# Weight sums loaded before a chunk ends, results made in pieces, relus put behind the next copy

## The chip, the cores and the metric

The kernel runs on one core of a Trainium2 chip. The metric is device time in microseconds, as the median of several runs. All inputs and outputs are 32-bit floats (the weights of the last two blocks arrive as 64-bit patterns and are narrowed on the chip).

## The reference, cut to what matters

Three blocks follow each other on a batch of 4 sequences of 576 rows and 512 features:

```
attn = thresholded softmax attention, 8 heads of 64                # block 1
X = real(fft(fft(x, axis=1), axis=2)); u = x + X                   # block 2
un = (u - mean(u)) / sqrt(var(u) + 1e-6)
y = u + relu(un @ w_ch1) @ w_ch2          # 512 -> 2048 -> 512
gate = sigmoid(causal conv of 5 taps over y)                       # block 3
out = (gate * (y @ w_val)) @ w_out
```

The change is in block 2's last line. The rows of all sequences, 4 x 576 = 2304, are cut there into chunks.

## The kernel before, in words

**Number format.** Every factor of a product is kept as a high and a low part, and a product is three passes: high x high, low x high, high x low. So a value that enters TensorE is first split: ScalarE makes the high part with a copy, and VectorE the rest with a subtraction.

**Chunks.** `CHUNKS` has 512, 384, 512, 512 and 384 rows. Chunk 0 is woven into the attention by a planner (`Loom`), which simulates the engines' clocks and picks which piece of work is emitted next. From chunk 1 on the order is written out in `mlp` (L1618 to L1676). Each engine runs its instructions in the order of emission, and so does SP, which issues nearly all DMAs. The planner goes on beside that with side work: the weight sums described below (`g_combine`), and narrowing the weights of block 3 (`g_load`, `g_convert`, L281 to L291).

**An ordinary chunk** (1 and 4) goes through 16 blocks of hidden features. `emit_h` (L1121) multiplies one block of `w_ch1` with the split rows `un`, then ScalarE takes the relu out of PSUM as `hh` and VectorE its remainder `hl`. `emit_c` (L1138) multiplies `w_ch2` with these into four PSUM accumulators, one block behind.

**A fast chunk** (2 and 3, `g_fast`, L1237) takes hidden blocks in pairs, in 8 steps, and saves products by a scheme in the manner of Strassen and Winograd: the chunk's rows are cut in two halves, and seven products of 256 columns do what eight would. The right-hand sides (`b11`, `b21`, `b22`, `t1` to `t4`, made by `g_blocks` on VectorE as differences and split by `split_block`, L1221) stay for the whole chunk; each set takes the room of a tile that stood for something else before. The left-hand sides are blocks of `w_ch1` and four sums of them, `s1` to `s4`. `g_combine` makes the sums during chunk 1 and stores them to DRAM. `fetch` (L1231) brings them back on SP, into a ring of five slots. One step has the products x (b11), y (b21), x (t2), zz (t1), x (t3), zz (b22), x (t4), where x and zz gather several products in one PSUM tile. Between these, ScalarE copies intermediate values out of PSUM (`copied`, L1286), VectorE adds (`added`, L1290), and `relu` (L1295) puts one instruction on ScalarE and one on VectorE. `fill` (L1246) puts 8 groups of three matmuls for `w_ch2` between the products; they belong to the step before, so the first step has none, and the last step's follow at the chunk's end. In the last step of chunk 2, `renew` splits each right-hand side for chunk 3 as soon as its last product is emitted.

**The norm.** The mean and variance of the next chunk are worked out beside the current one by a generator (`g_norm`, then `g_var`, L1056 to L1101), which `advance_norm` (L1585) moves on by one step when a due time is reached. The due times are counted on an estimate of TensorE's progress. In a fast chunk it is called once after each yield of `g_fast`, in an ordinary one before a fast chunk twice per block. Its scratch tiles come from a pool of four buffers (`cs`, L1018). Chunk 1's end forces it on until `centred`, and then splits all seven right-hand sides for chunk 2 (L1661 to L1665).

**A chunk's result** (`finish`, L1150): for each of four row groups of features, VectorE multiplies the accumulator with the norm's factor into a tile of the pool of the relus (two buffers), POOL adds the residual (`load_res`), and SP stores each run of rows to DRAM (two runs in chunks 1 to 3). It stands at once behind the chunk's last matmuls, ahead of the next chunk. Chunk 4 then starts block 3's gate: it loads rows of y through SP and runs the convolution on VectorE, between the blocks (`start_gate`, L1714).

## Time and profile before

| What | us |
|---|---|
| median of 3 runs (872.08 to 877.37) | 873.7 |
| the profiled execution, its own time | 876.9 |
| its span, first to last instruction | 875.1 |
| TensorE busy in it (94%) | 821.1 |
| VectorE busy (72%) | 631.7 |
| ScalarE busy (52%) | 452.4 |
| GpSimd busy (45%) | 396.2 |
| mean granted TensorE clock, as a share of full speed | 0.982 |

Times in the rows are microseconds from the span's start unless a view gives ns. PE is TensorE's matmuls, PEld its weight loads, DVE VectorE, ACT ScalarE, POOL GpSimd, SPq the queue that issues DMAs. A name like `hl<-ct,hh` is what an instruction writes and reads, by the tile's name at allocation: `cx` and `ct` are the kernel's temporaries in a fast chunk, `raw` and `unh`, `unl` also the right-hand sides, and `mlp_xu` the ring of fetched sums. Chunk 1 lies at 427 to 495, chunk 2 to 603, chunk 3 to 699, chunk 4 to 773.

### The profile page before, as it was taken

The page shows a single profiled execution, that of the slowest core. Times are in us where ns is not written, and L with a number is a line of the kernel's source. Part 1 is how long each engine was busy: PE and PEld are TensorE (multiplying, and loading weights), DVE is VectorE, ACT ScalarE, POOL GpSimd, SP SyncE. Part 2 cuts the span into 40 slices and gives each one's busy share as a digit, 9 for nine tenths or more (in the row PEclk, how much of TensorE's full clock was granted, in tenths as well). Part 3 has the DMA queues.
Part 4 walks back from the last instruction along what each step waited for, and adds up shares of the span by engine and source line. Part 5 has one row for each costly group of instructions (what it writes and reads, how often), then busy time and mean ns, then how long its engine had stood idle before and what let it go on. Part 6 is the DMA issues. An engine that isn't in the chain of part 4 may idle for free.

```text
span 875.1 us, 14989 instructions
## 1 busy us (share of the span) xinstructions
PE 821.1 (94%) x5164; PEld 663.7 (76%) x5164; DVE 631.7 (72%) x1370; ACT 452.4 (52%) x947; POOL 396.2 (45%) x456
## 2 busy tenths in 40 slices
PE   8989999999899999999999759997999989999998
PEld 6555566566555668888899758986799889998996
DVE  7999999889989997888688635656533466627740
ACT  5787777776777766544452325334423314234432
POOL 4557865895698476664443030303211111066421
PEclk9999999999999999999999969998999999999999
DMA  6376365456725389769146266646543132253111
GB/s 209 104 226 212 103 191 177 169 162 216 244 101 176 120 295 370 240 231 384 67 182 233 68 198 191 196 148 207 157 149 100 55 102 91 79 199 108 61 47 62
DMA packets 76459, 145.00 MB, mean 166 GB/s; under 512 B 14296, under 2 KB 24536, under 8 KB 76384
## 3 DMA queue, kind: packets, MB, share of 16 engines
q1 hardware_dynamic: 69040, 120.20, 40.6%
q0 software_dynamic: 7200, 23.86, 8.8%
q8 instruction: 41, 0.67, 0.3%
q14 instruction: 34, 0.28, 0.1%
q10 hardware_dynamic: 144, 0.00, 0.0%
HBM read 104.17 MB, written 39.86 MB: 165 GB/s over the span
## 4 chain that ended last, share of the span: by engine, by line
PE 60%; DVE 20%; issue 7%; ACT 6%; POOL 4%; DMA 2%; SPq 1%; DVEq 0%; POOLq 0%; ACTq 0%
PE c L1261 7%; DVE neg L766 6%; PE c L1147 6%; PE h L1131 6%; DVE p L783 6%; PE o L1776 5%; PE h L1496 5%; PE c L1532 5%; PE v L1758 5%; PE x L1271 4%; PE s L701 4%; PE f L458 3%; ACT e L772 2%; PE t L803 2%; PE zz L1271 2%
## 5 line engine op out<-in xcount | busy, mean ns | idle before, releaser
L791 POOL TENSOR_SCALAR p<-p,su 128x576 f32<-128x576 f32 x144 | 109.6, 771 | 86.8 <-DVE su L718 77.5
L772 ACT ACTIVATE e<-s,neg 128x576 f32<-128x576 f32 x144 | 102.2, 742 | 50.9 <-DVE neg L766 44.3
L783 DVE SCALAR_TENSOR_TENSOR p<-s,thr,e 128x576 f32<-128x576 f32 x144 | 112.5, 815 | 8.7 <-DVE thr L711 0.5
L766 DVE TENSOR_REDUCE neg<-s 128x1 f32<-128x576 f32 x144 | 102.5, 747 | 5.9 <-PE s L701 5.3
L701 PE MATMUL s<-kt,qt 64*128 64x288 f32 (+1 forms) x640 | 99.1, 441 | 6.9 <-DVE p L783 5.7
L701 PEld LDWEIGHTS s<-kt,qt 64*128 64x128 f32 (+1 forms) x640 | 46.0, 176 | 46.5 <-issue 16.1
L803 PE MATMUL t<-ident,p 128*128 128x128 f32 x464 | 68.9, 280 | 9.3 <-ACT m L820 6.6
L803 PEld LDWEIGHTS t<-ident,p 128*128 128x128 f32 x464 | 50.5, 140 | 30.7 <-issue 13.2
L291 POOL TENSOR_TENSOR ct<-raw 128x512 fp32r<-128x512 f32 x24 | 26.3, 1095 | 101.2 <-DVE raw L287 81.8
L458 PE MATMUL f<-m,v 128*64 128x320 f32 (+1 forms) x512 | 69.5, 411 | 0.0
L820 ACT ACTIVATE m<-t 128x512 f32<-128x512 f32 x116 | 65.6, 598 | 1.7 <-PE t L803 0.8
L1134 ACT ACTIVATE hh<-h 128x384 fp32r<-128x384 f32 x32 | 15.7, 490 | 76.8 <-PE h L1131 76.6
L458 PEld LDWEIGHTS f<-m,v 128*64 128x64 f32 x512 | 33.8, 137 | 27.3 <-ACT m L820 3.5
L1147 PE MATMUL c<-hl,w1h 128*128 128x384 f32 x128 | 43.6, 340 | 2.3 <-DVE hl L1135 2.3
L1156 POOL TENSOR_TENSOR res<-ht,res 128x512 f32<-128x512 f32 (+1 forms) x20 | 23.2, 1195 | 48.4 <-DVE ht L1155 48.4
L1147 PE MATMUL c<-hh,w1h 128*128 128x384 f32 x128 | 43.4, 339 | 0.0
L1147 PE MATMUL c<-hh,w1l 128*128 128x384 f32 x128 | 43.3, 339 | 0.0
L1732 DVE SCALAR_TENSOR_TENSOR acc<-ypad,cw,acc 128x288 f32<-128x288 f32 x96 | 43.0, 518 | 0.0
L1761 DVE TENSOR_TENSOR gvf<-v,gate 128x288 f32<-128x288 f32 x30 | 13.7, 456 | 39.2 <-PE v L1758 39.2
L1135 DVE SCALAR_TENSOR_TENSOR hl<-h,hh 128x384 fp32r<-128x384 f32 x32 | 17.8, 556 | 31.4 <-ACT hh L1134 31.4
L283 ACT ACTIVATE cx<-cx,wide_bias 128x512 int32<-128x512 int32 x40 | 28.9, 721 | 13.7 <-DVE cx L281 13.6
L1261 PE MATMUL c<-hh,w1h 128*128 128x512 f32 x88 | 34.8, 395 | 1.0 <-ACT hh L1299 1.0
(343 smaller groups left out, 2226.6 us busy)
## 6 DMA issues: line engine op xcount, KB each, us to landing
raw<-in_moe_w_ch POOLq DMA_DIRECT2D x32, 512.0 KB, 6.0
mlp_xu<-s SPq DMA_DIRECT2D x64, 256.0 KB, 3.6
qt<-in_q SPq DMA_DIRECT2D x15, 576.0 KB, 4.9
kt<-in_k SPq DMA_DIRECT2D x15, 432.0 KB, 3.6
s<-raw SPq DMA_DIRECT2D x12, 512.0 KB, 2.6
ypad<-y_d SPq DMA_DIRECT2D x16, 288.0 KB, 3.0
out<-os SPq DMA_DIRECT2D x18, 256.0 KB, 2.0
v<-in_v SPq DMA_DIRECT2D x16, 256.0 KB, 2.6
```

The source lines that it names most:

```text
L458: PE.matmul(out=f[h * 64:h * 64 + 64, 0:n], lhsT=w, rhs=r, start=(t == 0), stop=(t == 4))
L701: PE.matmul(out=s[o, c, 0:HALF], lhsT=qt[w, hh, q], rhs=kt[w, 2 if h == 2 and hh else hh], start=True, stop=True)
L766: DVE.tensor_reduce(out=neg[u][:, j, 0:1], in_=sc[g][:, :, 0:HALF], axis=AX.XY, op=ALU.max, negate=True)
L772: ACT.activation(e, sc[g][:, :, 0:HALF], AF.Exp, bias=neg[u][:, j, 0:1], scale=1.0)
L783: DVE.scalar_tensor_tensor(out=p_view(g).rearrange("p (a b) -> p a b", a=2), in0=sc.pop(g)[:, :, 0:HALF], scalar=thr[u][:, j:j + 1], in1=e ...
L791: POOL.tensor_scalar(out=v, in0=v, scalar1=ssum[u][:, j:j + 1], scalar2=1.0, op0=ALU.mult, op1=ALU.mult)
L803: PE.matmul(out=f[:, t, :], lhsT=pv[:, t * 128:(t + 1) * 128], rhs=ident, is_transpose=True, start=(t == 0), stop=(t == 3))
L820: ACT.activation(o, fv, AF.Copy)
L1131: PE.matmul(out=f[:, 0:n], lhsT=ww[:, k * 128:(k + 1) * 128], rhs=x[:, k, 0:n], start=(i == 0), stop=(i == 3 * KB - 1))
L1147: PE.matmul(out=ch[c][o][:, 0:n], lhsT=ww[:, o * 128:(o + 1) * 128], rhs=x, start=(at_ == 0 and i == 0), stop=(at_ == FB - 1 and i == 2))
L1261: PE.matmul(out=ch[c][o][:, 0:n], lhsT=ww[:, o * 128:(o + 1) * 128], rhs=y[:, 0:n], start=(first and i == 0), stop=(last and i == 2))
L1271: PE.matmul(out=f[:, 0:m], lhsT=ww[:, k * 128:(k + 1) * 128], rhs=x[:, k], start=(first and i == 0), stop=(i == 5), skip_group_check=not f ...
```

## The change

- `g_var` waits a due time of 1,400 behind each of four squares, where it waited 2,000 behind each second one.
- `finish` becomes a generator, `g_finish`, that yields ahead of each of its four pieces. Its product goes into a scratch tile of the norm's pool. Behind chunks 1 and 2 it is not run at once: the next chunk, a fast one, takes one piece at every second yield of its first step. The planner and the norm do nothing in that chunk until yield 14, early in its second step. Behind chunks 0, 3 and 4 it still runs at once.
- In `g_fast`, `renew` becomes `settle`, and is called only behind products that are followed by a copy out of PSUM, or an addition from it into a temporary. Three of the four relus of a step are put on a list (`later`) and emitted there, behind the next such copy; the splits for the next chunk come behind them, in the order in which their products ended.
- At the last block of chunk 1 the norm is forced on to `centred`, and b11, b21 and t2 are split, ahead of that block's matmuls. The other four splits stay ahead of the last `emit_c`, and `fetch(5)` follows them there.

```diff
@@ g_var
                 ACT.activation(sq[k], z[:, k], AF.Square)
-                if k % 2:
-                    yield 2000.0
+                yield 1400.0
@@ finish
+            for _ in g_finish(c):
+                pass
+
+        def g_finish(c):
             n = CHUNKS[c]
             acc, u, r = ch.pop(c), res.pop(c), rs.pop(c)
             for k in range(KB):
-                t = f32(got["h"].tile([128, NM], F32R, tag="h" + "hl"[k % 2], name="ht"))[:, 0:n]
+                yield
+                t = scratch(n)
                 DVE.tensor_tensor(out=t, in0=acc[k][:, 0:n], in1=r, op=ALU.mult)
@@ g_fast
-            def renew():
+            later = []
+
+            def settle():
+                while later:
+                    relu(*later.pop(0))
                 while over:
-                    name = over.pop()
+                    name = over.pop(0)
                     if end and c + 1 in FAST:
                         split_block(c + 1, name)
...
                 product(x, a11, "b11", True)
                 copied(x, tmp[0])
-                renew()
+                settle()
                 yield
                 y = ps_f.tile([128, 512], F32, tag="f", name="y")
                 product(y, a12, "b21", True)
-                relu(added(y, tmp[0]), 2 * p, 0)
-                renew()
+                added(y, tmp[0])
+                later.append((tmp[0], 2 * p, 0))
                 yield
                 fill(1)
-                renew()
                 yield
                 product(x, s2, "t2", False)
                 copied(x, tmp[1])
+                settle()
                 fetch(k0 + 6)
-                renew()
...
                 product(z, s4, "b22", False)
-                relu(added(z, tmp[1]), 2 * p, 1)
+                added(z, tmp[1])
+                later.append((tmp[1], 2 * p, 1))
                 fetch(k0 + 9)
-                renew()
...
                 product(x, a22, "t4", False)
-                relu(x[:, 0:m], 2 * p + 1, 0)
-                renew()
+                settle()
+                later.append((x[:, 0:m], 2 * p + 1, 0))
...
+            settle()
             rest.append(lambda: fill(2 * KB))
@@ the loop over chunks
-                for m in g_fast(c):
+                for n, m in enumerate(g_fast(c)):
+                    if n % 2 == 1 and next(left, "end") != "end":
+                        continue
+                    if n < 14:
+                        continue
                     loom.run(until=loom.now["PE"])
...
                 rest.pop()()
-                finish(c)
+                left = g_finish(c)
+                if c + 1 not in FAST:
+                    finish_rest(left)
                 continue
...
             for n, j in enumerate(js):
+                if c + 1 in FAST and n == FB - 1:
+                    while not centred:
+                        advance_norm(c, True)
+                    loom.run(lambda: ("combined", FB // 2 - 1) in loom.done)
+                    for name in ("b11", "b21", "t2"):
+                        split_block(c + 1, name)
                 emit_h(c, j)
...
                 if c + 1 in FAST:
-                    for name in ("b11", "b21", "t2", "t1", "t3", "b22", "t4"):
+                    for name in ("t1", "t3", "b22", "t4"):
                         split_block(c + 1, name)
+                    fetch(5)
...
-            finish(c)
+            left = g_finish(c)
+            if c + 1 not in FAST:
+                finish_rest(left)
```

## Rows read from the trace of the kernel before

**Rows 1.** Waits of TensorE, 495 to 785: us in total, times, longest.
```profile
PE x L1271 <- DMA mlp_xu<-s: 11.7, 1, 11.7
PE x L1271 <- ACT cx L1288: 8.4, 5, 4.4
PE x L1271 <- DVE raw L1226: 2.9, 1, 2.9
PE c L1147 <- DVE hl L1135: 2.3, 1, 2.3
```

**Rows 2.** Timeline of the SP queue at chunk 1's end: start, us, line, tiles, count.
```profile
480.67 5.65 SPq L1016 DMA_DIRECT2D res<-u_d  x8
...
504.61 4.03 SPq L1158 DMA_DIRECT2D y_d<-res  x8
508.81 2.52 SPq L1234 DMA_DIRECT2D mlp_xu<-s  x5
```

**Rows 3.** Stretches: length, busy of PE, PEld, DVE, ACT, POOL; clock; DMA share; GB/s.
```profile
488.40:495.35 6.95, 6.94 (x40) 6.53 (x38) 3.55 (x7) 1.58 (x4) 1.03 (x1) 1.00 0.00 0
495.35:513.27 17.92, 2.81 (x12) 2.34 (x13) 10.77 (x19) 5.70 (x11) 4.57 (x5) 0.60 0.35 102
513.27:519.60 6.33, 6.33 (x30) 6.33 (x31) 1.35 (x2) 2.23 (x5) 2.40 (x2) 0.53 0.92 304
710.10:713.50 3.40, 3.40 (x11) 3.40 (x12) 3.40 (x6) 0.00 (x0) 0.00 (x0) 0.55 0.00 0
```

**Rows 4.** Timeline of TensorE: first fill of chunk 2; chunk 3's first product and first fill.
```profile
521.05 0.40 PE L1261 MATMUL c<-hh,w1h 128*128 128x512 f32 x1
...
602.78 0.40 PE L1271 MATMUL x<-raw,w0h 128*128 128x256 f32 x2
...
617.13 0.50 PE L1261 MATMUL c<-hh,w1h 128*128 128x512 f32 x1 [0.98 <-ACT hh L1299]
```

**Rows 5.** Chain that ended last, one product in chunk 2: start, us, matmuls.
```profile
560.05 0.71 PE zz L1271 x6
```

**Rows 6.** Timeline across chunk 1's end, with idle time before and its releaser.
```profile
488.01 0.73 ACT L283 ACTIVATE cx<-cx,wide_bias 128x512 int32<-128x512 int32 x1 [0.96 <-DVE cx L281]
...
488.45 0.63 PE L1034 MATMUL mean<-cs,ones 128*128 128x512 f32 x2
...
493.81 2.48 DVE L1053 TENSOR_TENSOR z<-z,mean 128x512 f32<-128x512 f32 x4
...
495.81 0.51 PE L1271 MATMUL x<-raw,w0h 128*128 128x256 f32 x2 [0.46 <-ACT raw L1225]
...
497.65 0.63 ACT L1225 ACTIVATE raw<-cs 128x512 fp32r<-128x512 f32 x1 [0.70 <-DVE cs L1217]
...
498.74 1.29 DVE L1226 TENSOR_TENSOR raw<-z,raw 128x512 fp32r<-128x512 f32 x2
```

**Rows 7.** Timeline behind chunk 3: POOL's four additions, a remainder in chunk 4.
```profile
697.83 5.04 POOL L1156 TENSOR_TENSOR res<-ht,res 128x512 f32<-128x512 f32 x4 [27.09 <-DVE ht L1155]
...
709.50 0.55 DVE L1135 SCALAR_TENSOR_TENSOR hl<-h,hh 128x384 fp32r<-128x384 f32 x1
```

**Rows 8.** Single lines: ns minimum/median/maximum, first and last start, shapes.
```profile
L1155 DVE TENSOR_TENSOR ht<-c,nr x20: 547/691/692, 424.7 to 774.8; 128x512 f32<-128x512 f32 x12, 128x384 f32<-128x384 f32 x8
...
L1292 DVE TENSOR_TENSOR cx<-y,cx x16: 408/424/426, 504.8 to 683.3; 128x256 f32<-128x256 f32 x16
...
L1299 ACT ACTIVATE hh<-cx x20: 399/418/421, 505.3 to 678.8; 128x256 fp32r<-128x256 f32 x20
...
L1300 DVE SCALAR_TENSOR_TENSOR hl<-ct,hh x12: 412/425/3199, 518.7 to 689.6; 128x256 fp32r<-128x256 f32 x12
```

**Rows 9.** Timeline of VectorE and POOL in the first steps of chunks 2 and 3.
```profile
505.84 0.92 DVE L1300 SCALAR_TENSOR_TENSOR hl<-cx,hh 128x256 fp32r<-128x256 f32 x1 [0.61 <-ACT hh L1299]
...
613.09 3.20 DVE L1300 SCALAR_TENSOR_TENSOR hl<-ct,hh 128x256 fp32r<-128x256 f32 x1 [0.62 <-ACT hh L1299]
...
613.47 2.53 POOL L1083 TENSOR_TENSOR cs<-cs 128x512 f32<-128x512 f32 x2
```

More of the change, by code (lines that the diff above doesn't have):

```diff
@@ L1342, in g_fast @@
                 added(x, tmp[2])
+                settle()
                 fetch(k0 + 8)
-                renew()
                 yield
@@ L1347, in g_fast @@
                 relu(tmp[2], 2 * p + 1, 1)
-                renew()
                 yield
                 product(z, s4, "b22", False)
-                relu(added(z, tmp[1]), 2 * p, 1)
+                added(z, tmp[1])
+                later.append((tmp[1], 2 * p, 1))
                 fetch(k0 + 9)
-                renew()
                 yield
                 fill(1)
-                renew()
                 yield
                 product(x, a22, "t4", False)
-                relu(x[:, 0:m], 2 * p + 1, 0)
-                renew()
+                settle()
+                later.append((x[:, 0:m], 2 * p + 1, 0))
                 yield
                 fill(3)
-                renew()
                 yield
@@ L1366, in g_fast @@
                     q += [group(p, jx, 2 * p + i, o) for o in range(KB)]
+            settle()
             rest.append(lambda: fill(2 * KB))
@@ L1616, in mlp, with finish_rest @@
         gated = False
+        def finish_rest(g):
+            for _ in g:
+                pass
+        left = iter(())
         arena()
```

## The prediction

> **What bounds the kernel now.** I read the waits of TensorE first, then the SP queue, then the stretches and the timelines around the boundaries between chunks. TensorE is the engine that sets the end: in chunks 1 to 4 it hardly waits, and what it does wait for stands nearly all at boundaries [rows 1]. The reader is to see three places.
> - Chunk 1 to 2. The first weight sum is fetched only after the eight stores of chunk 1's result, because all of them stand on SP in order: stores from 504.61, fetches from 508.81 [rows 2], and TensorE sits 11.7 us for the landing. Before that it sat 2.9 us for a split. The clock then falls: granted 0.60 while it idles and 0.53 in the 6.33 us of work behind it, near the lower of its two levels, against 1.00 before [rows 3]. The first fill of the second step starts at 521.05 [rows 4].
> - Chunk 2 to 3. From the first product at 602.78 to the first fill at 617.13 are 14.35 us [rows 4]. An unfilled step is seven products of 0.71 us [rows 5], so 5.0; 4.4 of the rest is one wait for a copy out of PSUM that ScalarE made late.
> - Chunk 3 to 4. One wait of 2.3 us for the remainder of a relu [rows 1], with the clock at 0.55 for the 3.4 us behind it [rows 3].
>
> **The change part by part.**
>
> **Loads and splits ahead of chunk 1's end.** Everything that the loads need is now forced ahead of the last hidden block of chunk 1, and its planner comes later than before: with a due time of 1,400 behind each of four squares, where there were two of 2,000, counting the due times through chunk 1's 16 blocks puts the column mean's inputs at the sixteenth block, not the fourteenth. So they are emitted behind a conversion step that ends on ScalarE at 488.74 [rows 6]. Then a ScalarE copy (0.63, as for a split) and a two-input subtraction on VectorE (0.65, half of the pair of 1.29) make them: 490.0. TensorE would have started the mean at 488.45, so it waits 1.6. After the mean's 0.63 come, in order on VectorE, the centring (2.48), four differences (4 x 0.65) and three remainders of splits (3 x 0.65): 490.7 + 2.48 + 2.6 + 1.95 = 497.7. Only then comes the last hidden block's remainder, 0.55 [rows 7]: 498.3. Behind it on VectorE wait the four other splits and a few conversion instructions; behind it on TensorE stands the last output block. TensorE works at 0.174 us a matmul (6.95 for 40, [rows 3]); the 26 matmuls from there to that block's second are done by about 495.2, so it waits some 3.1 us more and leaves chunk 1 at 500.1, where it now starts chunk 2 at 495.81 [rows 6]. That is a loss of 4.3. In return SP has nothing ahead of the five fetches but the residual's loads, which are out by 486.3 [rows 2]; from the first issue to the end of TensorE's wait were 513.27 - 508.81 = 4.5 us [rows 2, 3], so they are there by 495, and the 11.7 goes.
>
> **The result in pieces.** The first step of chunks 2 and 3 now holds, on VectorE, three additions (0.42), three remainders (0.43) and four products of the pieces (0.55 at 384 columns, 0.69 at 512) [rows 8]: 4.75 or 5.3 us. VectorE starts when two products are done (1.5 us) and stands about 1.6 us for ScalarE: 1.1 for the second copy and the first relu, and 0.5 for the second relu, at 0.42 each [rows 8] and a tenth for a signal. So the first fill can start 7.9 (8.4) us after the first product. The norm waits until step two, where its squares took turns with the first step; that costs nothing, since the counted due times still put the last difference of chunk 3 just ahead of the last step.
> The pieces' additions on POOL now lie beside the remainders. A remainder took 0.92 in place of 0.43 beside such an addition, and 3.20 beside two others, ending with the second of them [rows 9]. The nearest row is the first, since it has the same POOL instruction: 0.5 for each of two remainders, 1.2 with some for the third. The ends are 0 and 3 x 2.8 = 8.3 per chunk. The Trainium skill, "SBUF — State Buffer", section "Who interferes with whom", speaks against this place: a VectorE instruction with two SBUF inputs and a GpSimd one that reads SBUF shut each other out for one whole instruction, so by it a hold is at most one addition, 1.26. By that rule the price could be up to 3.8 per chunk, and the sum would come out at 864; the 3.20 shows a longer hold than the rule gives.
> On SP two stores of each piece now stand between the fetches. The third fetch of the first step goes behind piece one's stores, about 6.4 us after the first product, and lands at 10.9 where it is wanted at 12.4; the next has some 2 us too. I cost them at nothing; without that cover each late microsecond counts in full.
>
> Boundary 1 to 2: 500.1 + 7.9 + 1.2 (POOL) + 0.5 (backlog of splits; 0 to 1.1) + 1.5 (clock) = 511.2 against 521.05: **9.9 less**. The clock's term: a wait of 2.3 was followed by 3.40 us at 0.55, which is 1.5 of lost work; the ends are 0 and half of 6.33, 3.0 [rows 3]. The ends of the whole are 13 and 0.6 less.
> Boundary 2 to 3: 8.4 + 1.2 = 9.6 against 14.35: **4.7 less**; ends 5.9 less and 2.4 more.
>
> **Each relu behind the next copy.** Four relus a step move; their number and length stay. Of the five waits for a copy, 8.4 us, one is the 4.4 already counted, and four are about 1 each [rows 1]. Two stand behind the logarithm and exponential of the norm, which are emitted as a pair after the step's first copy; they stay, since the relu of the step before now goes ahead of them. One stands behind the splits of chunk 2's last step, where the copy now goes ahead of relu and split: it goes. One is chunk 4's norm in chunk 3's last step; that part now comes so late that it falls into chunk 4, off the copies. **2.0 less**; ends 0 and 4.
>
> **Chunk 3's result at once, but from the scratch buffers.** Counting due times, chunk 4's norm is half done when chunk 3 ends and holds three of the four scratch buffers, so product and addition alternate: 4 x (0.69 + 1.26) = 7.8, where two buffers let POOL run its four through in 5.04 [rows 7], with one product of 0.69 ahead. The 2.1 more delay the stores, the loads of the gate behind them on SP, the gate's instructions and the hidden remainder behind those on VectorE, at 709.50 [rows 7], for which TensorE already waits. **2.0 more**; ends 0 (if buffers are free) and 4, twice that. At chunk 0's end the same buffers are free: nothing.
>
> **Sum:** -9.9 - 4.7 - 2.0 + 2.0 = -14.6. Made against the profiled execution's 876.9 that is 862.3. That execution lies 3.2 above the median of 873.7, inside the runs' 872.08 to 877.37, so against the median it is **859**.
>
> **The rivals.**
> - *The loads do not come early* (chance 0.12). If SP still holds the fetches (behind a store or a ring slot not yet free), the 9.9 falls away: 869. For it: SP is strictly in order, and pieces' stores are now among the fetches. Against: in the trace nothing but the residual's loads stands there in the last blocks of chunk 1 [rows 2].
> - *POOL holds VectorE in the first steps* (0.08; the other side). Place: the three remainders of the first step of chunks 2 and 3. Price: 2.8 each, as the row with 3.20 has it, 2 x 8.3 less the 2.4 counted, so 14.2; and 1.5 more twice, as the fills then wait long enough for the clock to fall: 876, slower than before. It decides the sign from a mean hold of some 2.4 us on. For it: that row. Against: the other row, with 0.5, is the one with these additions.
> - *No holds and no fall of the clock* (0.08): 859 - 2.4 - 1.5 - 0.5 = 854.6.
>
> **How the numbers follow.** The forecast has 0.72 and by its ends 852 to 867. A measurement of this kernel can tell about 1%, 8.7 us: faster means under 865. Nearly all of the forecast and all of the fourth case lie there, 0.79; the first rival and a tail of the forecast lie within 1%, 0.16; part of the second rival is beyond, 0.05. The range of 851 to 868 leaves out most of both other rivals.
>
> **What would show it.** Right: the first fill of chunk 2's second step comes about 10 us sooner, with fetches ahead of every store of chunk 1's result; TensorE waits at the mean (1.6) and at the last output block of chunk 1 (3.1); chunk 3's first fill comes 9 to 10 us after its first product; chunk 3's products and additions alternate singly. Wrong: a long wait for a fetched weight sum anywhere; remainders over 2 us in the first steps; waits for copies of 1 us left in the last step of chunk 2; or a new wait at the last step, where the last differences now come just in time.

## The result and the profile after

Four runs of the changed kernel had a median of **862.5 us** (862.13 to 866.53), four of the kernel before beside them 875.1 (872.08 to 877.37): ratio 0.9869, 95% interval 0.9824 to 0.9913. That is 3.5 us above the forecast of 859.0 and inside its range. The profiled execution took 862.13 with a span of 860.4 and a mean clock of 0.998; before, the span was 875.1 at 0.982, so the traces are 14.7 apart where the sum said 14.6. The medians are 12.6 apart: the profiled execution of the changed kernel is its fastest of four, that of the kernel before (876.9) one of its slower ones. And the terms behind that sum were off in both directions, as the stretches show (us, from the timelines of TensorE):

| stretch | before | after | difference | predicted |
|---|---|---|---|---|
| start to h of chunk 1's last block but one | 484.29 | 483.25 | -1.0 | 0 |
| from there to chunk 2's first fill | 36.76 | 23.11 | -13.7 | -9.9 |
| from there to chunk 3's first product | 81.73 | 83.45 | +1.7 | -1.0 |
| chunk 3's first product to its first fill | 14.35 | 8.50 | -5.9 | -4.7 |
| from there to chunk 4's start | 81.78 | 81.57 | -0.2 | -1.0 |
| chunk 4's start to the end | 176.19 | 180.52 | +4.3 | +2.0 |

The first stretch is not counted as a gain of the change: in the experiments below, whose work has the changed kernel's order up to there, that h starts anywhere from 481.6 to 483.5. The one trace before lies 0.8 above these, so a small gain is not excluded. Places near chunk 1's end are therefore compared by their distance from it.

The waits of TensorE from 480 to 785 us, the view of [rows 1] (us in total, times, longest):

```profile
PE c L1146 <- DVE hl L1134: 5.6, 2, 3.8
PE x L1275 <- ACT cx L1296: 2.5, 3, 1.0
PE v L1783 <- DVE gvf L1786: 1.6, 1, 1.6
PE c L1265 <- ACT cx L1307: 1.4, 1, 1.4
```

The 11.7 us for a weight sum and the 2.9 for a split are gone, and the waits for copies fell from 8.4 to 2.5. In their place stand waits for a hidden remainder (L1134, two of them), one behind chunk 4 (L1783) and one for a relu (L1307). The SP queue at chunk 1's end, the view of [rows 2]:

```profile
484.97 16.44 SPq L1238 DMA_DIRECT2D mlp_xu<-s  x6
503.83 0.80 SPq L1162 DMA_DIRECT2D y_d<-res  x2
...
509.07 0.39 SPq L989 DMA_DIRECT2D moe_w_val_h<-cx  x1
```

Six fetches stand ahead of the first store of the result now; before, all eight stores stood ahead of them. What replaces the wait is seen on TensorE at the same place, the view of [rows 4, 6] (start, us, the instruction, its idle time before and the releaser):

```profile
483.25 0.85 PE L1130 MATMUL h<-unh,w0h 128*128 128x384 f32 x4
...
488.27 0.50 PE L1034 MATMUL mean<-cs,ones 128*128 128x512 f32 x1 [0.70 <-ACT cs L1023]
...
494.44 0.44 PE L1146 MATMUL c<-hh,w1h 128*128 128x384 f32 x1 [0.76 <-ACT hh L1133]
...
496.88 0.45 PE L1146 MATMUL c<-hl,w1h 128*128 128x384 f32 x1 [1.82 <-DVE hl L1134]
...
498.75 0.39 PE L1275 MATMUL x<-raw,w0h 128*128 128x256 f32 x2
...
506.36 0.50 PE L1265 MATMUL c<-hh,w1h 128*128 128x512 f32 x1 [0.40 <-ACT hh L1307]
```

The two predicted waits are there, at the mean (0.70, and 0.23 more ahead of its second matmul, where 1.6 was forecast) and in the last output block (0.76 and 1.82, where 3.1 was forecast). The first product comes 15.5 behind that h, where 15.8 was forecast (500.1 on a timeline with h at 484.29). The step from first product to first fill takes 7.61. At chunk 3, the same two rows and the longest remainder between them:

```profile
589.81 0.40 PE L1275 MATMUL x<-raw,w0h 128*128 128x256 f32 x2
...
598.31 0.50 PE L1265 MATMUL c<-hh,w1h 128*128 128x512 f32 x1 [0.95 <-ACT hh L1307]
```
```profile
595.40 1.48 DVE L1308 SCALAR_TENSOR_TENSOR hl<-ct,hh 128x256 fp32r<-128x256 f32 x1 [0.48 <-ACT hh L1307]
```

### The profile page after: what moved, and what is told of

The parts are those of the page before. It is cut to its first block, busy times and chain, and to the rows that moved or that the text cites. A ratio compares the mean times of both kernels' runs of the same rounds, so it can differ in the third digit from the quotient of the medians.

```text
span 860.4 us, 14973 instructions
## 1 busy us (share of the span) xinstructions
PE 816.7 (95%) x5164; PEld 658.1 (76%) x5164; DVE 633.6 (74%) x1370; ACT 450.2 (52%) x947; POOL 396.6 (46%) x456
## 4 chain that ended last, share of the span: by engine, by line
PE 61%; DVE 18%; issue 7%; ACT 6%; POOL 4%; DMA 2%; SPq 1%; DVEq 0%; POOLq 0%; ACTq 0%
PE c L1146 7%; PE c L1265 7%; PE h L1130 6%; DVE neg L766 6%; DVE p L783 5%; PE o L1801 5%; PE h L1500 5%; PE c L1536 5%; PE v L1783 5%; PE s L701 4%; PE f L458 4%; PE x L1275 4%; ACT e L772 2%; PE t L803 2%; PE f L588 2%
## 5 line engine op out<-in xcount | busy, mean ns | idle before, releaser
L803 PEld LDWEIGHTS t<-ident,p 128*128 128x128 f32 x464 | 50.5, 140 | 30.7 <-issue 13.7
L1160 POOL TENSOR_TENSOR res<-cs,res 128x512 f32<-128x512 f32 (+1 forms) x20 | 23.4, 1196 | 38.6 <-DVE cs L1159 38.6
L1296 ACT ACTIVATE cx<-x 128x256 f32<-128x256 f32 x32 | 12.2, 380 | 46.8 <-PE x L1275 46.8
L1134 DVE SCALAR_TENSOR_TENSOR hl<-h,hh 128x384 fp32r<-128x384 f32 x32 | 17.8, 555 | 25.0 <-ACT hh L1133 25.0
```

The costliest lines, as they stand in the source:

```text
L803: PE.matmul(out=f[:, t, :], lhsT=pv[:, t * 128:(t + 1) * 128], rhs=ident, is_transpose=True, start=(t == 0), stop=(t == 3))
```

## The experiments

Each was timed beside the kernel before, which had a median of 875.1 or 875.4 and, beside kernels 11 and 12, a single run of 873.4. Ratios are to these. Kernels 7, 11 and 12 have one run each; runs of one kernel differ by up to 5 us (kernel 6: 864.64 to 869.62), so these three are read by their stretches and not by their times.

| kernel | us (median) | ratio, 95% interval |
|---|---|---|
| the changed kernel | 862.54 | 0.9869, 0.9824 to 0.9913 |
| 1 no early fetch | 863.49 | 0.9858, 0.9836 to 0.9880 |
| 2 results at once | 862.95 | 0.9866, 0.9847 to 0.9884 |
| 3 old queue order (1 and 2) | 869.97 | 0.9937, 0.9923 to 0.9952 |
| 4 norm at the end | 863.81 | 0.9860, 0.9845 to 0.9874 |
| 5 splits behind h | 861.39 | 0.9835, 0.9821 to 0.9850 |
| 6 relus back | 867.81 | 0.9912, 0.9892 to 0.9931 |
| 7 no additions | 857.97 | one run |
| 8 own tiles | 859.23 | 0.9811, 0.9792 to 0.9831 |
| 9 own tiles, splits behind h | 856.64 | 0.9772, 0.9755 to 0.9789 |
| 10 the same, planner runs | 854.28 | 0.9762, 0.9728 to 0.9797 |
| 11 at once, two tiles | 856.06 | one run |
| 12 at once, planner runs | 867.21 | one run |

### What took the 11.7 us away (1, 2, 3)

**1.** The fetch ahead of chunk 1's end is taken out; the first step of chunk 2 fetches itself.

```diff
                     for name in ("t1", "t3", "b22", "t4"):
                         split_block(c + 1, name)
-                    fetch(5)
```

> Against the changed kernel's 862.5. Theory: the fetches were late only because the stores of chunk 1's result stood ahead of them on SP; taking the result apart clears SP by itself, so the fetch at the first step's own place is issued just as early, with the first at about 485: 862.5, within 2, and no wait for a fetched sum. Rival: the fetch written ahead of chunk 1's last block is what takes the 11.7 away: 870 or more, and the wait for the fetched sum is back.

**2.** The results of chunks 1 and 2 are made at once again; the early fetch stays.

```diff
-                left = g_finish(c)
-                if c + 1 not in FAST:
-                    finish_rest(left)
+                finish(c)
```
(at both places where a chunk ends)

> Results of chunks 1 and 2 made at once again, the early splits and the early fetch kept. Theory (each of the two is enough against the 11.7): no wait for the first fetched sum, but the next fetches stand behind the stores again and VectorE makes four products first: 1 to 4 more than the changed kernel, 863.5 to 866.5, chunk 3's first fill 10 to 12 after its first product in place of 8.5. Rival (the pieces are what pays): 872.

**3.** Both edits together.

> The fetch of the sixth to eighth weight sums ahead of chunk 1's end is taken out and the results of chunks 1 and 2 are made at once, both together; the early norm and splits of chunk 1 and the later relus stay. Theory (either of the two puts the weight sums ahead of the eight stores of y on SP's queue, and that order is the whole gain at the boundary from chunk 1 to 2): the wait of a product for a weight sum comes back at 9 to 12 us in chunk 2's first step, the first fill of chunk 2 lies at 516 to 521 in place of 506 to 509, and the time is 871 to 875 us. Rival (the early norm and splits or VectorE's freed time made the gain, and the order on SP is a side matter): the first fill stays before 510 and the time at 862 to 866 us.

Measured: 863.49, 862.95 and 869.97. With either alone the six (or five) fetches still stand ahead of the stores; with both gone, the SP queue and TensorE's wait are back. The queue of kernel 3, and the wait and first fill on its TensorE:

```profile
501.71 3.88 SPq L1162 DMA_DIRECT2D y_d<-res  x8
505.77 11.12 SPq L1238 DMA_DIRECT2D mlp_xu<-s  x9
```
```profile
511.08 1.62 PE L1275 MATMUL x<-raw,mlp_xu 128*128 128x256 f32 x6 [10.16 <-DMA mlp_xu<-s]
...
518.62 0.40 PE L1265 MATMUL c<-hh,w1h 128*128 128x512 f32 x1
```

The fetches are issued behind the stores at 505.77, TensorE waits 10.16, and the first fill comes 36.3 us behind the last h but one (482.31 here), as before the change, so **the order on SP is the cause of the gain at this boundary**, and the early fetch is redundant as long as no store stands in front. The time came out 1 us below the expected 871, the mechanism as expected. The order is worth 7.4 us of the time (869.97 against 862.54) and not the whole 13.2 of this stretch, since kernel 3 is 2.9 faster from there to chunk 3's first product and 1.6 faster in chunk 3's first step. In kernel 2 part of the wait comes back later, where the sums behind the fifth go out behind the eight stores:

```profile
510.85 1.22 PE L1275 MATMUL zz<-unh,mlp_xu 128*128 128x256 f32 x4 [4.24 <-DMA mlp_xu<-s]
```

Half of what chunk 2 loses by it, 3.1 us from its first fill on, is made up at chunk 3's start: the 10 to 12 us expected for that step did not come, it takes 6.90, 1.6 less than in the changed kernel (below).

### What the early norm and splits are worth (4, 5)

**4.** The block ahead of chunk 1's last hidden block is taken out, and all seven splits follow the last block as before.

```diff
-                if c + 1 in FAST and n == FB - 1:
-                    while not centred:
-                        advance_norm(c, True)
-                    loom.run(lambda: ("combined", FB // 2 - 1) in loom.done)
-                    for name in ("b11", "b21", "t2"):
-                        split_block(c + 1, name)
                 emit_h(c, j)
...
-                    for name in ("t1", "t3", "b22", "t4"):
+                    for name in ("b11", "b21", "t2", "t1", "t3", "b22", "t4"):
```

> The centring of chunk 2 and the splits of its first three blocks go back behind h of chunk 1's last block; fetch, pieces and relus stay as in the changed kernel. Theory (the early splits only move a wait: the last c stands for hh and hl, 0.8 and 1.8 us, and the mean for 0.7, where the first product stood 2.9 for its split sum): the waits of the mean, of the last c for hh and hl go to under 0.3 each, a product of the first step waits 2.5 to 4.5 us for a split sum, the first fill lies within 1 us of the changed kernel's 506.4 to 508.8, time 861 to 864.5 us. Rival (the early splits are worth what they start sooner, about 3 us of VectorE's seven splits): the first fill is 2 to 3 us later and the time 865 to 867 us.

**5.** Norm early, but the three splits behind the last hidden block.

```diff
                     loom.run(lambda: ("combined", FB // 2 - 1) in loom.done)
-                    for name in ("b11", "b21", "t2"):
-                        split_block(c + 1, name)
                 emit_h(c, j)
+                if c + 1 in FAST and n == FB - 1:
+                    for name in ("b11", "b21", "t2"):
+                        split_block(c + 1, name)
```

> Only the splits of the first three blocks of chunk 2 go behind h of chunk 1's last block, so that hh and hl stand ahead of them on ScalarE and VectorE; the centring stays early. Theory (1.8 and 0.8 us of waits of the last c are the price of those splits in front of hl, and with the waits the fall of the clock behind them goes): c waits under 0.3 for hh and hl, the clock from 495 to 505 is 1.0, the first product starts 2 to 3 us earlier (495.8 to 497.0), the first fill at 503.5 to 505.5, time 858.5 to 861 us. Rival (the splits themselves set the start, so the wait only moves to the first product): a product waits 1.5 to 3 us for a split sum, the first fill stays at 506 to 509, time 861.5 to 863.5 us.

Kernel 4 took 863.81 and has the old wait again; a mean also waits 1.06:

```profile
498.91 0.80 PE L1275 MATMUL x<-raw,w0h 128*128 128x256 f32 x2 [2.92 <-DVE raw L1230]
...
507.82 0.50 PE L1265 MATMUL c<-hh,w1h 128*128 128x512 f32 x1
```

Its h of the last block but one starts at 482.93, so the first fill comes 24.9 behind it: 23.1 in the changed kernel, 25.8 in kernel 1, which has the changed kernel's order of work there but, as kernel 4 here, a fallen clock behind its waits (last section). So the early splits moved a wait and gained nothing that can be told, as the first theory had it, though its mean waits more than the 0.3 expected. Kernel 5:

```profile
493.51 0.44 PE L1146 MATMUL c<-hl,w1h 128*128 128x384 f32 x1 [1.03 <-DVE hl L1134]
...
495.37 0.39 PE L1275 MATMUL x<-raw,w0h 128*128 128x256 f32 x2
...
500.31 0.74 PE L1275 MATMUL zz<-unh,mlp_xu 128*128 128x256 f32 x4 [1.18 <-ACT ct L1296]
...
504.55 0.50 PE L1265 MATMUL c<-hh,w1h 128*128 128x512 f32 x1 [0.38 <-ACT hh L1307]
```

The wait for hh is gone and that for hl falls from 1.82 to 1.03 (not to the expected 0.3, because the centring still stands in front). The last h but one starts at 481.69, so the first product comes 13.7 behind it in place of 15.5, but the first fill 22.9 in place of 23.1: the start is 1.8 earlier, and a wait of 1.18 for a copy and others take it back. That is the rival's case, with the wait at a copy and not at a split sum. Against kernel 1, whose clock fell (25.8), it is some 3 us less. Behind the shorter wait the clock stayed at 1.00 here, and also in kernels 9 and 10, which have this edit; but it stayed there in four of nine kernels without the edit too (last section), so three executions do not show that the edit is the reason. The time, 861.39, lies between the two expectations, and its interval overlaps the changed kernel's.

### What the relu order and the pieces are worth (6, 7, 11, 12)

**6.** Each relu follows its sum at once, as before.

```diff
-                later.append((tmp[0], 2 * p, 0))
+                relu(tmp[0], 2 * p, 0)
...
-                later.append((tmp[1], 2 * p, 1))
+                relu(tmp[1], 2 * p, 1)
...
-                settle()
-                later.append((x[:, 0:m], 2 * p + 1, 0))
+                relu(x[:, 0:m], 2 * p + 1, 0)
+                settle()
```

> Each relu again at once behind its addition or product, all else as changed. The prediction's step, that the move takes 2.0 off: 864.5 (2 more than the changed kernel). Theory from the trace after, where chunk 2 from its first fill to its end took 83.4 in place of 81.7, with new waits of 1.4 and 1.0 behind relus: the move gains nothing or costs: 860 to 862.5.

It took 867.81, 5.3 more than the changed kernel: **my theory here fell**. Chunk 2 from first fill to chunk 3's first product takes 87.53 against 83.45, and the remainder of chunk 3 82.76 against 81.57; from chunk 3's first product to its first fill it is 0.5 less. A further 1.1 lies ahead of chunk 2's first fill, where the clock of this execution fell (last section) and the relus need not be the cause. The waits for copies from 505 to 680 us:

```profile
PE x L1275 <- ACT cx L1296: 7.1, 5, 2.1
```

Five waits with 7.1 us where the changed kernel has three with 2.5. The longest, 2.14, ends at 536.84, and the granted clock of the stretch from 535 to 545 us is 0.83, so this late copy was paid twice.

**7.** POOL's residual additions of chunks 1 and 2 are left out.

```diff
-                POOL.tensor_tensor(out=u[k][:, 0:n], in0=t, in1=u[k][:, 0:n], op=ALU.add)
+                if c + 1 not in FAST:
+                    POOL.tensor_tensor(out=u[k][:, 0:n], in0=t, in1=u[k][:, 0:n], op=ALU.add)
```

> The changed kernel without POOL's eight residual additions of chunks 1 and 2 (these chunks' result lacks the residual). Theory (the additions lengthen a few of VectorE's splits of hidden activations beside them, 1.06 and 1.48 us in place of 0.42 to 0.55, but little of it reaches TensorE): those splits take 0.4 to 0.6 us, the stretch from the first product to the first fill of chunk 2 is 7.2 to 7.6 us where the clock is 1.0, and of chunk 3 7.4 to 8.1 in place of 8.5; span 858.5 to 861.5 us with the clock as in the changed kernel. Rival (the additions hold VectorE up at the price that the sum gave them, 1.2 us in each chunk): 7.3 or less in chunk 3 and 858 us or less.

The time, 857.97 with a span of 856.2, is within the rival's bound and under the theory's, but the step in question took 7.44, inside the theory's range by 0.04 and over the rival's 7.3. So neither expectation holds whole. The same remainder as the 1.48 above, and chunk 3's two rows on TensorE (a line of the file is added, so L1308 reads L1309 here):

```profile
592.91 0.43 DVE L1309 SCALAR_TENSOR_TENSOR hl<-ct,hh 128x256 fp32r<-128x256 f32 x1 [0.48 <-ACT hh L1308]
```
```profile
587.34 0.40 PE L1276 MATMUL x<-raw,w0h 128*128 128x256 f32 x2
...
594.78 0.50 PE L1266 MATMUL c<-hh,w1h 128*128 128x512 f32 x1
```

Without the additions the step takes 7.44 in place of 8.50: they cost 1.06, near the sum's 1.2, which was the rival's price. Another 2.9 of the saving lies in chunk 2 behind its first fill, where a conversion on VectorE waits 2.1 us for its buffer, not 5.3 (below, kernel 10). The store that holds this buffer is issued only 0.7 earlier (508.39 against 509.07), so most of the shorter wait is a shorter way from issue to release, 4.7 in place of 7.0 us; why, no run shows.

**11.** Edit 2 (results at once), and into the two tiles of h, as before.

```diff
                 yield
-                t = scratch(n)
+                t = f32(got["h"].tile([128, NM], F32R, tag="h" + "hl"[k % 2], name="ht"))[:, 0:n]
```

> As with the results of chunks 1 and 2 at once, but all results are multiplied into the two tiles of h, as in the kernel before, in place of the four scratch buffers. Theory (four free buffers let VectorE's four products run through, 2.74 us, where with two it stands 2 us for POOL): the stretch from chunk 3's first product to its first fill is 8.4 to 9.5 us in place of 6.9; at chunk 4 and its end the 3.3 us of the scratch buffers come back. Rival (the buffers do not matter at the boundary from chunk 2 to 3): 6.9 to 7.5 us.

**12.** Edit 2 (results at once, from the scratch buffers), and the planner, which stands still for the first 14 turns of a chunk in the changed kernel, runs in them.

```diff
                     if n < 14:
+                        loom.run(until=loom.now["PE"])
                         continue
```

> As with the results of chunks 1 and 2 at once (scratch buffers), but the planner also runs in the first step of a chunk, so that a conversion's instructions stand ahead of the first addition of chunk 3 as in the kernel before. Theory (the 4.4 us wait for a copy in the kernel before came from that conversion on ScalarE and VectorE, and the planner's pause took it away, not the pieces): the stretch of chunk 3 is 10 to 14 us in place of 6.9. Rival (the pause does not matter; the later relus or the four buffers took the wait away): 6.9 to 8.7 us.

From chunk 3's first product to its first fill kernel 2 takes 6.90, kernel 11 6.90, kernel 12 9.11. So in kernel 11 the rival held: VectorE does stand for POOL with two tiles, but TensorE's first fill is no later for it. VectorE of kernel 11, the third product:

```profile
590.48 0.69 DVE L1159 TENSOR_TENSOR ht<-c,nr 128x512 f32<-128x512 f32 x1 [0.72 <-POOL res L1160]
```

In kernel 12 a conversion's three instructions are back ahead of the first addition, and beside POOL's additions they take 0.95, 1.52 and 1.75 us:

```profile
596.31 0.95 DVE L281 TENSOR_SCALAR cx<-raw 128x512 int32<-128x512 int32 x1
597.19 1.52 DVE L282 TENSOR_SCALAR ct<-raw 128x512 int32<-128x512 int32 x1
598.63 1.75 DVE L285 SCALAR_TENSOR_TENSOR cx<-raw,cx 128x512 int32<-128x512 int32 x1
```

That is 2.2 of the 7.45 us between 14.35 and 6.90; the expected 10 to 14 was too much, so the planner's standstill is one cause and not the only one. Kernel 6, with the relus back and the standstill kept, takes 7.96. No kernel had the old relus and the running planner together, so the other 5 us are not split by a run, but the trace of the kernel before says what they are made of. First the whole step there (from 602.78) and in kernel 2 (from 591.56; columns as in [rows 3]), then TensorE's wait of the kernel before and what stood ahead of that copy on VectorE and ScalarE:

```profile
602.78:617.13 14.35, 8.95 (x55) 8.51 (x53) 9.88 (x13) 5.56 (x13) 10.07 (x9) 0.76 0.62 178
591.56:598.46 6.90, 6.79 (x55) 6.55 (x54) 3.96 (x8) 2.75 (x8) 3.98 (x4) 1.00 0.45 151
```
```profile
610.29 1.22 PE L1271 MATMUL x<-unh,mlp_xu 128*128 128x256 f32 x4 [4.42 <-ACT cx L1288]
```
```profile
605.62 0.89 DVE L281 TENSOR_SCALAR cx<-raw 128x512 int32<-128x512 int32 x1
```
```profile
606.54 0.72 ACT L283 ACTIVATE cx<-cx,wide_bias 128x512 int32<-128x512 int32 x1 [2.41 <-DVE cx L281]
...
608.53 1.13 ACT L1078 ACTIVATE cs<-z 128x512 f32<-128x512 f32 x2
```

The same matmuls kept TensorE busy for 8.95 us and not 6.79, because the granted clock is 0.76 and not 1.00: so 2.2 of the 7.45 us are the price of the clock. The rest are two waits, 4.42 and 0.98. The late copy stood behind the conversion, two squares of the norm (1.1) and a relu (0.4). The conversion itself starts 2.84 behind the chunk's first product, in kernel 12 only 0.81: with two tiles, VectorE's last two products ahead of it had waited 1.46 and 0.55 for POOL. So the two tiles, which cost TensorE nothing in kernel 11, do seem to cost where a conversion stands behind them; this is read from two traces, and no run tested it. What is settled is that **the pieces are not the cause**: without them the step is 1.6 shorter. Kernel 12 also waits 6.1 us for a weight sum that is fetched behind eight stores and a conversion's two.

### What the scratch buffers cost at the end (8)

**8.** Where a result is made at once (chunks 0, 3 and 4), it goes into h's two tiles as before.

```diff
-                t = scratch(n)
+                t = f32(got["h"].tile([128, NM], F32R, tag="h" + "hl"[k % 2], name="ht"))[:, 0:n] if c + 1 not in FAST else scratch(n)
```

> Results that are made at once (chunks 0, 3 and 4) again in the two buffers of the relus' pool; pieces in the scratch tiles as changed. Theory: products and additions alternate singly because the scratch buffers are taken, and the 3.8 and 0.6 of TensorE's waits early in chunk 4 and the 1.6 behind it come from that: 858.5 to 860.5, POOL's four additions behind chunk 3 in 5.0 in place of 7.6. Rival: the gate's instructions hold the remainder anyway: 862.5, within 1.

It took 859.23, and 175.33 from chunk 4's start to the end in place of 180.52, as the theory had it. The changed kernel's POOL behind chunk 3 and its TensorE in chunk 4 and at its end:

```profile
678.80 1.29 POOL L1160 TENSOR_TENSOR res<-cs,res 128x512 f32<-128x512 f32 x1 [13.82 <-DVE cs L1159]
680.89 1.29 POOL L1160 TENSOR_TENSOR res<-cs,res 128x512 f32<-128x512 f32 x1 [0.81 <-DVE cs L1159]
```
```profile
693.73 0.69 PE L1146 MATMUL c<-hl,w1h 128*128 128x384 f32 x1 [3.76 <-DVE hl L1134]
...
761.21 0.80 PE L1783 MATMUL v<-y0h,wvh 128*128 128x288 f32 x4 [1.61 <-DVE gvf L1786]
```

And POOL and TensorE of kernel 8, whose chunk 4 starts at 682.37 (679.88 in the changed kernel):

```profile
681.29 5.04 POOL L1160 TENSOR_TENSOR res<-ht,res 128x512 f32<-128x512 f32 x4 [13.82 <-DVE ht L1159]
```
```profile
693.87 0.45 PE L1146 MATMUL c<-hl,w1h 128*128 128x384 f32 x1 [2.29 <-DVE hl L1134]
```

One run of four additions against four single ones with gaps of 0.81: VectorE's first gate instruction comes 8.0 behind the chunk's start, not 10.6; the wait for the remainder is 2.29, not 3.76, and the one at 761 is gone, as is one of 0.58 for a padding row. These are 3.7 of the 5.2 us. The rest goes with the clock, which is 0.58 in the 3.5 us behind the wait in the changed kernel and 1.00 in kernel 8; behind nearly the same wait it was 0.55 in the kernel before [rows 3]. By the medians the edit gives 3.3.

### The best version (9, 10)

**9.** Edits 5 and 8 together.

> Both the splits behind h of chunk 1's last block and, where a result is made at once, the tiles of h in place of the scratch buffers. Theory (the two prices lie at different ends of the chunks and add: 2 to 3 and 3.3 us): 855 to 857.5 us, waits for hl at the gate's start 2.3 us as with own tiles alone. Rival (the splits' wait only moves): 858.5 to 860 us, as with own tiles alone.

**10.** Kernel 9 with the planner running in the first step, the edit of kernel 12.

> On top of own tiles and splits behind h: while the pieces of a chunk's result are made, the planner that places the conversions of the next weights also runs, so that the store of the converted weight goes out ahead of the pieces' stores on SP. Theory (the wait of a fill for a relu, 2.4 us at 519.7 in that kernel, comes from VectorE standing 6.3 us in front of a conversion whose buffer is held by that late store): the store is issued at 502 to 504 in place of 509, VectorE's stand is under 1 us, that fill's wait under 0.5 us, time 853.5 to 855.5 us. Rival (the conversion's instructions now come ahead of the first additions of a chunk, at chunk 3's start above all, and take back what the store gives): a product or fill of chunk 3's first step waits 1.5 to 4 us more, time 856 to 859 us.

856.64 and **854.28**, both in their theories' range, and the second is the lowest median here. The intervals of the two overlap, so their times alone do not settle which is faster. What kernel 10 mends is read in kernel 9, on SP, VectorE and TensorE:

```profile
509.04 0.38 SPq L989 DMA_DIRECT2D moe_w_val_h<-cx  x1
```
```profile
517.10 0.43 DVE L281 TENSOR_SCALAR cx<-raw 128x512 int32<-128x512 int32 x1 [6.32 <-DMA moe_w_val_h<-cx]
```
```profile
519.68 0.50 PE L1265 MATMUL c<-cx,w1h 128*128 128x512 f32 x1 [2.44 <-ACT cx L1307]
```

The two parts of the converted weight were made by 497.6 and 501.9, but their stores stood on SP behind the stores of the pieces, because the planner that emits them stands still for the first step; the buffer of the high part stayed taken, the next conversion stopped VectorE for 6.3 us, and a fill waited 2.4. In kernel 10 the high part goes out at 497.64 and the low one at 501.88 (502 to 504 was expected), ahead of the pieces, and the conversion waits for nothing:

```profile
497.64 0.32 SPq L989 DMA_DIRECT2D moe_w_val_h<-cx  x1
```
```profile
510.70 0.42 DVE L281 TENSOR_SCALAR cx<-raw 128x512 int32<-128x512 int32 x1
```

Chunk 2 from first fill to chunk 3's first product takes 80.77 in place of 85.30: the wait of 2.44 is gone, and so is a granted clock of 0.61 in the 4.3 us behind it. The rival's price is there too, but small: chunk 3's first step 8.73 in place of 8.49.

## Why the prediction was right, and where its sizes were not

- **Loads ahead of the stores on SP.** Right, and shown by kernels 1 to 3. The term was -9.9 and came to -13.7. The waits at chunk 1's end were 3.5 in place of 4.7, but the first product was only 0.3 earlier than forecast. Of the rest, 2.0 is the step itself, 7.61 in place of 7.9 + 1.2 + 0.5: no backlog of splits reached it, and one remainder was held there (1.06), not two or three. The other 1.5 is the fall of the clock, which this execution did not have. Kernel 1, with the same work there, had it: first fill 25.8 behind the last h but one, where the forecast makes 26.9 and the changed kernel 23.1.
- **The result in pieces.** The 9.6 forecast for chunk 3's first step was 8.50, and POOL's share in it 1.06 against 1.2. But I credited the pieces with the gain, and kernels 2 and 11 reach 6.90 without them. Of the 14.35 before it named 5.0 of products and 4.4 of waiting; the clock of 0.76 in that step, 2.2 us, it did not see. The sentence that failed is "I cost them at nothing", of the stores between the fetches: it looked at the fetches alone. With the planner at a standstill, the conversion's store is queued behind the same stores, and it costs the 1.40 that the changed kernel waits at 518.66, most of the 1.7 by which chunk 2 grew; in kernel 10, with pieces and a running planner, that wait is gone.
- **POOL beside VectorE.** The Trainium skill, "SBUF — State Buffer", section "Who interferes with whom", has a VectorE instruction with two SBUF inputs and a GpSimd one that reads SBUF shut each other out for one whole instruction. In the first steps the trace agrees: a remainder took 1.06 and 1.48 in place of 0.42, longer by less than one addition (1.29). The rival that built on the 3.20 of [rows 9] did not come in the first steps. The 864 that the rule's bound gave is near the measured 862.5, but not for its reason, since the additions cost 1.06 in chunk 3 and not 3.8. And a long hold is still there in the second step of chunk 2, beside two instructions of the norm on POOL:

```profile
521.38 3.22 DVE L1308 SCALAR_TENSOR_TENSOR hl<-cx,hh 128x256 fp32r<-128x256 f32 x1 [0.92 <-ACT hh L1307]
```
```profile
521.79 2.52 POOL L1082 TENSOR_TENSOR cs<-cs 128x512 f32<-128x512 f32 x2
```

That is 2.8 longer than 0.42, more than one such instruction (1.26), so here the measurement differs from the page, and it decides. TensorE's next wait comes 8 us behind it.
- **Relus behind the next copy.** Sign right, size 2.0 against 5.3 by kernel 6, of which 1.1 may be the clock's. In the table little of it is left, since the conversion's late store stands in the same stretches: with that store early, the changed relus give what was forecast in one chunk of two: kernel 10's chunk 2 takes 80.77 from its first fill on, 1.0 below before, as forecast; in chunk 3 it gains 0.4 (81.38 against 81.78), not 1.0. The two waits that the prediction saw go are gone (0.99 at 590.84 and 0.94 at 686.97 of the kernel before), and a new one of 0.88 stands at 602.66. That the 11.7 us of standstill had given ScalarE and VectorE time to catch up, and that late copies cost more without it, would explain the rest; no run tested that alone.
- **Scratch buffers.** Sign right, +2.0 against +4.3 (by kernel 8 5.2, of which 3.7 are waits and the rest the clock). The wait behind chunk 3 rose by 1.4, with 0.6 for a padding row beside it; what I left out is that chunk 4's own result uses the same buffers, two of which the gate holds, and waits 1.6 there.

That the total was right to 0.1 in the traces is luck: terms that were too small on either side nearly cancel, 1.0 of the gain lies in the first stretch, for which nothing was forecast, and the two traces lie 2.1 further apart than the medians. In the medians the gain is 12.6, 2.0 less than the sum. The other 1.4 of the 3.5 us by which 862.5 lies above the forecast are the base: the kernel before had 875.1 beside the changed one, not 873.7.

## What to carry to other kernels

A strictly ordered queue is a hidden dependence: before a store is moved or split, list every transfer behind it on that queue, also those of side work (here a conversion's store whose buffer blocks another engine), and ask who waits for each landing. Where one change has several parts, take each out alone and then in pairs: here two parts each sufficed for the large gain, and one of them, the pieces with their buffers, cost more than it gave by a single run (kernel 11, without either, took 856.06).

## What the runs showed of the hardware

The same instructions with the same waits were followed by different clocks. The changed kernel and kernel 1 have the same order of work at chunk 1's end and wait 0.76 and 1.82 us there; the stretches are those from 495 to 500 and 500 to 505 us (length, busy of PE, PEld, DVE, ACT, POOL; clock; DMA share; GB/s), first the changed kernel, then kernel 1:

```profile
495.00:500.00 5.00, 3.18 (x22) 3.12 (x22) 5.00 (x10) 2.33 (x5) 1.50 (x1) 1.00 0.00 0
500.00:505.00 5.00, 4.66 (x39) 4.45 (x38) 3.79 (x9) 1.53 (x5) 3.64 (x3) 1.00 0.21 59
```
```profile
495.00:500.00 5.00, 3.39 (x11) 3.39 (x12) 5.00 (x10) 1.72 (x4) 1.77 (x1) 0.59 0.00 0
500.00:505.00 5.00, 5.00 (x33) 5.00 (x32) 1.66 (x4) 1.46 (x4) 1.40 (x1) 0.72 0.08 17
```

At 0.59 and 0.72 the clock spent part of both stretches at the lower level, and the way from the last output block's wait to the first fill took 3.36 + 8.83 in place of 1.87 + 7.61: 2.7 us. The times of kernel 1's four runs fit this: 861.03 at a mean clock of 0.998, 863.3 to 864.5 at 0.996 and 0.993. Of the nine kernels with these two waits (the changed one and 1, 2, 3, 6, 7, 8, 11, 12), the profiled execution shows a fall there in five (1, 3, 6, 7, 8) and none in four. (In kernel 11, one of the four, it falls later in the same step: 0.66 from 504 to 509.) So a term for the clock is a chance as well as a size, and here it goes with about 3 us of a single run. In kernels 5, 9 and 10, whose wait there is one of 1.03 to 1.06, the clock stayed at 1.00 from 490 to 515; three executions are too few to say that the shorter wait is the reason.
